# Linear attention and a gated feed-forward on one core: a new order of steps, with most tail loads moved to SyncE's queue

## The chip, the core and the metric

The kernel runs on one core of a Trainium2 chip. Five engines work side by side, each through its own list of instructions in order: PE (matrix products), DVE (vector), ACT (scalar functions and copies), POOL (here almost only an issuer of DMAs) and SP (SyncE, which only issues DMAs). They wait for each other and for DMAs through semaphores. The metric is the device time of one execution in microseconds, as the median of several runs.

## What is computed

```python
# q, k, v: (8 batches, 8 heads, 576 rows, 64), float32
q_p, k_p = phi(q), phi(k)              # phi(x) = where(x > 0, x, exp(x) - 1) + 1
kv  = einsum('bhsd,bhse->bhde', k_p, v)
z   = sum(k_p, axis=2)
num = einsum('bhsd,bhde->bhse', q_p, kv)
den = einsum('bhsd,bhd->bhs', q_p, z)[..., None] + 1e-06
x   = (num / den).transpose(0, 2, 1, 3).reshape(4608, 512)
out = ((x @ w1) * (x @ w2) @ w3) @ w_out     # w1, w2: 512x1024, w3: 1024x1024, w_out: 1024x512
```

The output is 4608x512 in float32.

## The kernel before

Each batch has 576 rows. The first 512 of them are its main part, handled as four blocks of 128 (j = 0 to 3); the last 64 are its tail. The main part of q, k or v of one batch is loaded in two halves of 512 KB (four heads each), the tail in small DMAs of 64 KB: four for q and k together, two for v. A chunk of the feed-forward is the 512 main rows of one batch (chunks 0 to 7); chunk 8 is made of all eight tails. w3 and w_out are multiplied together at the start, so that the second half of the feed-forward is one product with `wf_sb`.

All work is written as steps, and a table (`ORDER`) lists them in the order in which they are recorded. Scheduling is manual: each engine executes its instructions in the order of the table, and a step puts instructions into several engines' lists at once. A `+` behind a step chooses the other engine: POOL and not SP for a load, DVE and not ACT for most copies. The steps that matter here, with batch or chunk b:

- `Lb.g`, `Mb.g`, `Nb.g`: load half g of k, q, v (`load_qkv`, L104). `Rb.0` and `Rb.1`: load the tails of q and k, and of v (`load_tail`, L114). The buffers are pools of 13 halves and of 3 tails of each kind; a load waits for the buffer's last reader.
- `x`, `y`, `z` (k) and `X`, `Y`, `Z` (q): the three parts of phi on ACT (L179) and DVE (L184, L204, L209). `vb.i`: cast of a v half (L215) or tail (L221).
- `Kb`: the product of k and v of a batch (`kvp`, L245, L249) and its copy to `kv` (L254). It needs both halves and the tails of k and v of its batch.
- `Tb.0`: transpose of phi(q) by a DMA on SP (L269). `Ab.j`: one block of rows times kv (`nd`, L310), divided on DVE (L324 to L326); j = 4 is the tail. `Db.p`: transpose of the result by a DMA on SP (`xt`, L351).
- `Fc.f`: one eighth of the gated first layer of chunk c, eight matmuls into `a_ps` and `b_ps` (L362), an ACT copy (L367) and a DVE product (L368). Chunks 6, 7 and 8 use other steps for it, `Gc.q.i`: Strassen-like units of four or eight matmuls (L422), whose sums and products run on ACT (L450, L458) and DVE (L454, L459, L465). `e` and `d` make the sums of weights and of x that they need (L396, L407).
- `Oc.m`: one quarter of the second layer (eight matmuls into `o_ps`, L536, and a copy, L538). `S`, `H` and `Q` store the output.

PE, DVE and ACT take their work from the same table, and so do the two issuers of DMAs. SP's queue holds the halves, the transposes and the stores in the order of the table; when the DMA at its head waits for a buffer or for data, all behind it wait as well. POOL's list after the start holds only tails. So a tail on POOL never stands in front of a half or of a transpose in its issuer's list, and a tail on SP does.

`GATES` adds two waits by hand: the load `R6.0` waits for the landing of `T3.0`, and `M2.1` for `B0.0`.

Of the kernel before, what the change touches and what calls it, by code (L numbers as in the profile page):

```python
# [20 lines left out]
def kernel(  # L21
# [568 lines left out]
    A3.2 F2.0 M5.1 Y5.1 R5.1+ R4.1+ y4.2 S1.1 F2.2 M4.1 A3.1 R5.0+ D3.0 x4.2 z4.2 M4.0 F2.1 Y4.1  # L590
    N4.1 F2.4 R6.1+ L4.1 e0.0 A2.4 v4.2 L4.0 F2.6 e0.2 F2.7 X5.1 Z5.1 A3.4 F3.3 X4.0 Y4.0 Z4.0 O2.3+
    X4.1 y5.2 v4.1 y4.1 F3.1 y6.2 Z4.1 x4.1 F3.4 z4.1 v5.2 y4.0 x4.0 F3.0 N4.0 z4.0 F3.5 v4.0 O2.2+
    M5.0 X5.0 K4 v6.2+ e0.1 T4.0 F3.7 x5.2 z5.2 L5.1 x5.1 Y5.0 Z5.0 y5.1 F3.2 S0.0 A4.1 F3.6 L5.0
    y5.0 O2.1 N5.0 x5.0 A4.0 v5.0 O2.0 z5.1 N5.1 S2.1 A4.2 T5.0 v5.1 O3.3 z5.0 A4.3 D4.0 O3.2+ K5
    S3.1 O3.1 A5.3 M6.1 O3.0 A5.0 F4.0 X6.1 A5.2 F4.7 M6.0 X6.0 Y6.0 Z6.0 D3.1 F4.2 F4.4 A5.1 F4.5
    e1.0 F4.3 L6.1 y6.1 x6.1 A4.4 R7.0 L6.0 y6.0 y7.2 D5.0 F4.1 x6.0 F4.6 z6.0 Y6.1 Z6.1 F5.6 x6.2
    z6.2 z6.1 F5.5 N6.1 v6.1 N6.0 A5.4 e1.1 e1.3 M7.0 X7.0 F5.7 S2.0 F5.4 Y7.0 O4.2+ v6.0 K6 O4.3
    T6.0 A6.3 S3.0 O4.0 A6.1 F5.3 D5.1 x7.2 z7.2 A6.0 M7.1 Y7.1 R7.1 X7.1 Z7.1 N7.0 v7.0 L7.0 F5.1
    F5.0 A6.2 L7.1 Z7.0 F5.2 x7.1 y7.1 O4.1 y7.0 A6.4 e0.3 x7.0 z7.0 S4.1 z7.1 O5.0+ v7.2 N7.1 v7.1
    D6.0 d6.2 O5.1 K7 d6.0 d6.1 d6.3 G6.1.1 e1.2 T7.0 G6.0.1 G6.0.2 G6.1.2 m6.0.2 G6.1.3 G6.0.3  # L600
    G6.1.4 A7.3 S4.0 G6.0.4 G6.0.5 G6.1.5 S5.0 G6.2.4 G6.0.6 G6.0.7 G6.1.6 G6.1.7 m6.1.6 A7.0 m6.0.6
    G6.2.1 G6.2.2 G6.3.1 G6.2.3 G6.3.2 G6.3.3 G6.2.5 G6.3.4 G6.2.6 G6.3.5 G6.2.7 A7.4 G6.3.6 G6.3.7
    O5.2 m6.3.2 D1.1 A7.2 O5.3 m6.1.2 m6.2.6 D7.1 d8.0 d8.1 d8.3 G8.0.1 G8.0.2 d8.2 A7.1 G8.1.1
    G8.0.3 m6.3.6 G8.0.4 G8.1.3 G8.0.5 m8.0.5 G8.1.4 m6.2.5 G8.3.4 S5.1 D7.0 G8.1.5 G8.0.7 m6.2.2
    G8.2.4 G8.0.6 m8.0.6 G8.1.7 O6.0 m6.3.5 m6.1.5 m6.0.5 O6.3 d7.2 G8.2.1 G8.2.2 m8.2.2 d7.0 G8.3.1
    G8.2.3 G8.1.6 G8.3.3 G8.2.5 G8.3.2 G7.0.4 G8.3.5 G8.2.7 G8.3.6 m8.3.6 m8.1.6 G7.1.4 G8.3.7
    m8.0.2 O6.2+ S6.1 d7.1 d7.3 O6.1 S6.0 m8.2.5 G7.0.1 m8.3.5 G8.1.2 m8.1.5 m8.1.2 G7.1.1 G7.0.3
    G7.0.6 G7.1.3 G7.0.5 G7.2.4 G7.1.5 G8.2.6 G7.0.7 G7.1.6 G7.1.7 G7.0.2 m8.2.6 m8.3.2 m7.1.6
    G7.2.1 G7.2.2 G7.3.1 G7.2.3 G7.3.2 m7.0.5 G7.3.4 G7.3.3 G7.2.5 G7.3.6 G7.3.5 G7.2.7 G7.1.2
    G7.2.6 G7.3.7 m7.0.2 m7.2.5 O8.2 O8.3 m7.3.2 H8.3 m7.3.5 m7.2.2 O8.0 m7.1.2 m7.0.6 O8.1+ H8.2  # L610
    S8.0 O7.0 O7.1 S7.0 m7.2.6 m7.3.6 m7.1.5 O7.2+ H7.2 Q7.3
# [118 lines left out]
```

## Time and profile before

| | us |
|---|---|
| Median of 3 runs (248.71 to 250.32) | 249.44 |
| Profiled execution, whole | 247.36 |
| Its span, first to last instruction | 245.6 |
| PE busy | 229.7 (94%) |
| DVE busy | 184.7 (75%) |
| ACT busy | 136.4 (56%) |
| POOL busy | 44.8 (18%) |
| HBM traffic | 38.80 MB read, 9.44 MB written, 196 GB/s over the span |
| SP's queue (q1) | 36.71 MB, 55.4% of 16 DMA engines |
| POOL's queue (q0) | 12.33 MB, 25.1% of 16 DMA engines |

Busy time is the union of an engine's instructions; a PE that the page shows as busy has matmuls in flight, which need not be a PE without small waits. The span is counted from the first instruction; the profiled execution is 1.8 us longer than its span. All windows below are microseconds from the span's start.

### The profile page before, as it was taken

To read this page: it belongs to the slowest core of one execution; us is meant where nothing else is said; L and a number is where in the kernel's file an instruction comes from. 1 tells how busy PE (TensorE), PEld (TensorE's weight loads), DVE (VectorE), ACT (ScalarE), POOL (GpSimd) and SP (SyncE) were. 2 spreads that over 40 slices of the span, in tenths; PEclk is the share of its full clock that TensorE was granted. 3 is DMA by queue.
4 is the path that set the end of the run, shared out by engine and by line. 5 is a ranking of instruction groups with operands and counts; after the bars stand their busy time and mean duration, and the time that the engine had idled before them with its cause. 6 is when DMAs were issued, how large, how long until landed. Compare 5 with 4: busy or idle time off the path is not lost.

```text
span 245.6 us, 4278 instructions
## 1 busy us (share of the span) xinstructions
PE 229.7 (94%) x1548; PEld 133.2 (54%) x1548; DVE 184.7 (75%) x425; ACT 136.4 (56%) x222; POOL 44.8 (18%) x73
## 2 busy tenths in 40 slices
PE   0689968999999999999999999999999999999994
PEld 0345555654454554444545444454498686788542
DVE  3227979677698837989794589958999996989721
ACT  2207777658775715498663456736776285455220
POOL 8445467660000096200000000000000000000000
PEclk9999997999999999999999999999999999999999
DMA  6999999999869799798997989989980151040074
GB/s 152 192 201 299 297 250 243 198 274 280 274 126 350 152 247 313 166 348 225 275 308 153 256 221 242 280 231 328 209 247 0 23 144 29 0 175 0 3 171 171
DMA packets 65461, 49.43 MB, mean 201 GB/s; under 512 B 34016, under 2 KB 60384, under 8 KB 65440
## 3 DMA queue, kind: packets, MB, share of 16 engines
q1 hardware_dynamic: 54560, 36.71, 55.4%
q0 software_dynamic: 10736, 12.33, 25.1%
q8 instruction: 12, 0.20, 0.3%
q10 hardware_dynamic: 144, 0.13, 0.2%
q14 instruction: 9, 0.07, 0.1%
HBM read 38.80 MB, written 9.44 MB: 196 GB/s over the span
## 4 chain that ended last, share of the span: by engine, by line
PE 83%; DMA 13%; ACT 2%; issue 1%; POOL 0%; ACTq 0%; POOLq 0%
PE o_ps L536 25%; PE a_ps L362 17%; PE b_ps L362 17%; PE gu L422 9%; PE gt L422 6%; DMA q<-in_q_dram 5%; DMA k<-in_k_dram 5%; PE nd L310 4%; DMA wt_sb<-in_moe_w_out_dram 3%; PE kvp L245 2%; ACT e L179 1%; PE o_ps L561 1%; PE kvp L249 1%; PE xtp L341 1%; POOL w3b L137 0%
## 5 line engine op out<-in xcount | busy, mean ns | idle before, releaser
L536 PE MATMUL o_ps<-wf_sb,ab 128*128 128x512 bf16 x280 | 64.7, 379 | 0.0
L362 PEld LDWEIGHTS <-w_sb 128*128 128x128 bf16 x384 | 36.6, 98 | 40.2 <-issue 0.6
L362 PE MATMUL a_ps<-xt,w_sb 128*128 128x512 bf16 x192 | 50.8, 382 | 0.0
L362 PE MATMUL b_ps<-xt,w_sb 128*128 128x512 bf16 x192 | 50.2, 379 | 0.0
L536 PEld LDWEIGHTS <-ab 128*128 128x128 bf16 x280 | 26.9, 98 | 29.1 <-DVE ab L465 0.3
L368 DVE TENSOR_TENSOR ab<-a_sb,b_ps 128x512 bf16<-128x512 f32 x48 | 32.4, 684 | 13.0 <-PE b_ps L362 6.5
L367 ACT COPY a_sb<-a_ps 128x512 f32<-128x512 f32 x48 | 27.5, 585 | 21.5 <-PE a_ps L362 20.2
L538 ACT COPY o_sb<-o_ps 128x512 f32<-128x512 f32 x27 | 15.6, 586 | 34.6 <-PE o_ps L536 24.9
L326 DVE TENSOR_TENSOR xn<-nd,r 128x512 bf16<-128x512 f32 x30 | 20.7, 691 | 1.0
L422 PEld LDWEIGHTS <-spare 128*128 128x128 bf16 x192 | 18.6, 97 | 2.4
L179 ACT ACTIVATE e<-q 128x1024 bf16<-128x1024 f32 x16 | 16.8, 1058 | 5.0 <-DMA q<-in_q_dram 4.9
L310 PE MATMUL nd<-kv,qt 128*128 128x130 bf16 (+1 forms) x160 | 15.9, 221 | 2.8 <-DVE xn L326 1.7
L454 DVE TENSOR_TENSOR spare<-spare,gt 128x512 f32<-128x512 f32 x24 | 16.0, 682 | 2.8 <-ACT spare L450 2.3
L310 PEld LDWEIGHTS <-qt 128*128 128x128 bf16 (+1 forms) x160 | 11.5, 99 | 11.6 <-DVE xn L326 3.0
L154 PE MATMUL wf_ps<-wt_sb,w3t 128*128 128x512 bf16 x64 | 16.1, 394 | 1.1 <-DMA wt_sb<-in_moe_w_out_dram 0.8
L179 ACT ACTIVATE e<-k 128x1024 bf16<-128x1024 f32 x16 | 16.9, 1060 | 0.2 <-DMA k<-in_k_dram 0.2
L450 ACT COPY spare<-gu 128x512 f32<-128x512 f32 x24 | 13.4, 590 | 3.4 <-PE gu L422 2.8
L422 PEld LDWEIGHTS <-w_sb 128*128 128x128 bf16 x144 | 14.0, 98 | 2.4
L465 DVE TENSOR_TENSOR ab<-spare 128x256 bf16<-128x256 f32 x36 | 13.7, 419 | 0.1
L114 POOL DMA_DIRECT2D qk32r<-in_q_dram x12 | 7.6, 636 | 33.5 <-ACT o_sb L538 30.9
L324 DVE TENSOR_SCALAR r<-nd 128x8 f32<-128x8 f32 (+1 forms) x38 | 6.1, 162 | 10.0 <-PE nd L310 9.9
L209 DVE TENSOR_TENSOR qj<-e,y 128x512 bf16<-128x512 bf16 x32 | 12.1, 421 | 1.7 <-ACT e L179 0.9
(87 smaller groups left out, 301.9 us busy)
## 6 DMA issues: line engine op xcount, KB each, us to landing
out_dram<-o_sb SPq DMA_DIRECT2D x15, 512.0 KB, 4.3
q<-in_q_dram SPq DMA_DIRECT2D x13, 512.0 KB, 6.8
k<-in_k_dram SPq DMA_DIRECT2D x12, 512.0 KB, 6.9
v<-in_v_dram SPq DMA_DIRECT2D x12, 512.0 KB, 7.7
w3b<-in_moe_w_dram POOLq DMA_DIRECT2D x8, 256.0 KB, 10.1
k<-in_k_dram POOLq DMA_DIRECT2D x4, 512.0 KB, 8.5
w_sb<-in_moe_w_dram POOLq DMA_DIRECT2D x8, 256.0 KB, 7.8
q<-in_q_dram POOLq DMA_DIRECT2D x3, 512.0 KB, 11.0
```

Of the source, the lines that this page charges most:

```text
L154: nc.tensor.matmul(wfs[i], w3ts[i][:, kc, :], wo_sb[:, kc, :], start=(kc == 0), stop=(kc == FC - 1))
L179: nc.scalar.activation(out=e, in_=x, func=AF.Exp)
L310: nc.tensor.matmul(nds[g][rows, i * 2 * E1:(i + 1) * 2 * E1], w, kvs[b % 2][:, i, g].rearrange("p u e -> p (u e)"), start=True, stop=True)
L326: nc.vector.tensor_tensor(out=dst.rearrange("p (g h) e -> p g h e", g=2), in0=v4[:, :, :, 0:D], in1=r[rows].unsqueeze(3).to_broadcast([n, ...
L362: nc.tensor.matmul(ps, w[:, kc, f * P:(f + 1) * P], xt_of(c)[:, :, kc, :], start=(kc == 0), stop=(kc == KC - 1))
L367: nc.scalar.copy(out=a_sb, in_=a_ps)
L368: nc.vector.tensor_mul(out=abs_[c][:, f, :], in0=a_sb, in1=b_ps)
L422: nc.tensor.matmul(t[:, w], l, r, start=(first and w == 0 and k == 0), stop=(k == 1), skip_group_check=True)
L454: nc.vector.tensor_tensor(out=s, in0=o, in1=t, op=ALU.add)
L465: (nc.gpsimd if alt else nc.vector).tensor_mul(out=abs_[c][:, f, r * HN:(r + 1) * HN], in0=s[:, 0], in1=s[:, 1])
L536: nc.tensor.matmul(o_ps, ab[:, f, m * P:(m + 1) * P], wf_sb[:, f, :], start=(f == 0), stop=(f == FC - 1))
L538: copy_of(alt)(out=rows_of(c, m // 2)[:, m % 2], in_=o_ps)
```

## The change

Only the table changes. It keeps its 594 steps, and the first 165 of them are as they were (up to `x2.2`, behind the first two gated units of chunk 1). From there the steps stand in another order, and 28 of them have the other engine flag. Eight tail loads lose their `+` and so move from POOL to SP: `R2.1`, `R3.1`, `R4.0`, `R4.1`, `R5.0`, `R5.1`, `R6.0`, `R6.1`. Only `R2.0` and `R3.0`, which stand before the cut, stay on POOL; `R7.0` and `R7.1` were on SP already. Of the copies and casts, `O2.2`, `O2.3`, `O3.2`, `O4.2`, `O6.2`, `O7.2`, `O8.1`, `v2.1` and `v3.2` go from DVE to ACT, and `O1.1`, `O3.0`, `O3.1`, `O5.1`, `O6.3`, `O8.2`, `v4.0`, `v6.1`, `v7.0`, `v7.1` and `K7` from ACT to DVE. `GATES` stays.

```diff
-    A1.4 x2.1 F1.7 F1.6 x2.2 y2.2 z2.2 N2.1 y3.2 x3.2 O0.3 F1.0 Y2.0 X2.0 Z2.0 N2.0 y2.1 F1.1 v2.1+
-    R2.1+ z2.1 L2.0 y2.0 v2.2 F1.5 R3.1+ x2.0 z2.0 M3.0 v2.0 F1.4 O0.2 X3.0 K2 Y3.1 v3.2+ Z3.1 O0.1
...
+    A1.4 x2.1 F1.7 F1.6 x2.2 L2.0 y2.1 z2.1 M3.0 O0.3 X2.0 y2.2 F1.4 N2.0 N2.1 x2.0 O0.0 z2.2 x3.2
+    Y2.0 Z2.0 y2.0 R2.1 F1.1 Y3.1 Z3.1 v2.0 T2.0 z2.0 v2.1 y3.2 F1.2 Y3.0 L3.0 v2.2 L3.1 X3.0 z3.2
...
```

What this does to the lists of the issuers is clearest between the transposes of q of batch 4 and of batch 5. On SP, before (qt is the transpose of q, k32 and v32 are halves, out_0_dram the store of an output):

```order
L269 DMA_TRANSPOSE qt_1553<-qj_1308 128x18x128
L104 DMA k32_1571<-in_k_dram 128x4x256
L546 DMA out_0_dram<-o_sb_1010 128x1024
L104 DMA k32_1618<-in_k_dram 128x4x256
L104 DMA v32_1633<-in_v_dram 128x4x256
L104 DMA v32_1660<-in_v_dram 128x4x256
L546 DMA out_0_dram<-o_sb_1434 128x1024
L269 DMA_TRANSPOSE qt_1672<-qj_1393 128x18x128
```

and in the changed kernel (qk32r and v32r are tails):

```order
L269 DMA_TRANSPOSE qt_1475<-qj_1295 128x18x128
L104 DMA k32_1518<-in_k_dram 128x4x256
L104 DMA k32_1542<-in_k_dram 128x4x256
L114 DMA qk32r_1599<-in_q_dram 64x4x64 x2
L114 DMA qk32r_1599<-in_k_dram 64x4x64 x2
L546 DMA out_0_dram<-o_sb_1179 128x1024
L104 DMA v32_1619<-in_v_dram 128x4x256
L114 DMA v32r_1633<-in_v_dram 64x4x64 x2
L104 DMA v32_1648<-in_v_dram 128x4x256
L269 DMA_TRANSPOSE qt_1653<-qj_1472 128x18x128
```

Between the two transposes stand six tail DMAs more, all of them ahead of the last v half of batch 5, and one store less. POOL's list ended with these tails before; none of its rows is left in the changed kernel:

```order
L114 DMA qk32r_1103<-in_q_dram 64x4x64 x2
L114 DMA qk32r_1103<-in_k_dram 64x4x64 x2
L114 DMA qk32r_1144<-in_q_dram 64x4x64 x2
L114 DMA qk32r_1144<-in_k_dram 64x4x64 x2
L114 DMA v32r_1266<-in_v_dram 64x4x64 x2
L114 DMA v32r_1269<-in_v_dram 64x4x64 x2
L114 DMA qk32r_1299<-in_q_dram 64x4x64 x2
L114 DMA qk32r_1299<-in_k_dram 64x4x64 x2
L114 DMA v32r_1342<-in_v_dram 64x4x64 x2
```

These are the tails of batches 4, 5 and 6; the v tails of batches 2 and 3, which stood ahead of them, are gone from POOL as well, and those of batch 7 are on SP in both kernels. The third place is DVE's list in the G units of chunk 6. Before (gu_2408 is the bank into which units 5 and 7 of quarter 2 write on PE; spare are operands and sums, ab products, nd, r and xn the division of one block of attention):

```order
L326 TENSOR_TENSOR xn_2342<-nd_2398,r_2403 128x512
L465 TENSOR_TENSOR ab_2290<-spare_2301 128x256
L454 TENSOR_TENSOR spare_2299<-spare_2299,gt_2414 128x512
L454 TENSOR_TENSOR spare_2298<-spare_2298,gt_2431 128x512
L454 TENSOR_TENSOR spare_2296<-spare_2301,gu_2408 128x512
```

and in the changed kernel, where the same bank is gu_2401:

```order
L326 TENSOR_TENSOR xn_2326<-nd_2386,r_2391 128x512
L454 TENSOR_TENSOR spare_2278<-spare_2278,gt2_2340 128x512
L454 TENSOR_TENSOR spare_2280<-spare_2279,gt2_2346 128x512
L454 TENSOR_TENSOR spare_2282<-spare_2277,gt_2418 128x512
L465 TENSOR_TENSOR ab_2271<-spare_2282 128x256
L465 TENSOR_TENSOR ab_2271<-spare_2280 128x256
L454 TENSOR_TENSOR spare_2277<-spare_2281,gu_2401 128x512
```

Between the division and the addition that reads this bank stand two products and three additions, where one product and two additions stood.

More of the change, by code (lines that the diff above doesn't have):

```diff
@@ L585 @@
     M2.1 M3.1 A1.3 F0.3 P1.3 X2.1 R2.0+ A1.0 L2.1 h0 h1 Y2.1 P1.0 M2.0 h2 h3 Z2.1 i0 i1 X3.1 R3.0+
-    A1.4 x2.1 F1.7 F1.6 x2.2 y2.2 z2.2 N2.1 y3.2 x3.2 O0.3 F1.0 Y2.0 X2.0 Z2.0 N2.0 y2.1 F1.1 v2.1+
-    R2.1+ z2.1 L2.0 y2.0 v2.2 F1.5 R3.1+ x2.0 z2.0 M3.0 v2.0 F1.4 O0.2 X3.0 K2 Y3.1 v3.2+ Z3.1 O0.1
-    Y3.0 Z3.0 T2.0 A2.3 F1.2 A2.2 N3.0 F1.3 v3.0 L3.1 z3.2 L3.0 x3.0 x3.1 y3.0 S0.1 y3.1 O0.0 N3.1
-    T3.0 A2.1 R6.0+ v3.1 O1.1 z3.0 A2.0 O1.0 D2.0 R4.0+ S1.0 z3.1 K3 O1.2 A3.0 O1.3 A3.3 F2.5 F2.3
@@ L590 @@
[L590 to L611, printed above, removed]
+    A1.4 x2.1 F1.7 F1.6 x2.2 L2.0 y2.1 z2.1 M3.0 O0.3 X2.0 y2.2 F1.4 N2.0 N2.1 x2.0 O0.0 z2.2 x3.2
+    Y2.0 Z2.0 y2.0 R2.1 F1.1 Y3.1 Z3.1 v2.0 T2.0 z2.0 v2.1 y3.2 F1.2 Y3.0 L3.0 v2.2 L3.1 X3.0 z3.2
@@ new lines @@
+    Z3.0 F1.0 K2 e0.0 R3.1 O0.1 A2.3 x3.0 O0.2 A2.1 S0.0 y3.0 F1.3 A2.2 v3.2 N3.1 y3.1 F1.5 N3.0
+    T3.0 A2.0 x3.1 z3.1 v3.1 z3.0 O1.1+ e1.0 v3.0 D2.0 O1.0 e1.1 e1.3 S1.0 K3 O1.2 D1.1 A3.1 M4.1
+    O1.3 A3.2 F2.0 A3.0 F2.7 F2.1 X4.1 e1.2 A3.3 e0.2 M4.0 X4.0 F2.6 Y4.0 Z4.0 F2.3 A2.4 F2.2 F2.4
+    Y4.1 Z4.1 L4.1 x4.1 y4.1 z4.1 R4.0 F2.5 N4.0 v4.0+ x4.2 S0.1 y4.2 z4.2 D3.0 M5.1 X5.1 R4.1 F3.0
+    v4.2 L4.0 y4.0 x4.0 z4.0 A3.4 F3.2 Y5.1 O2.2 N4.1 M5.0 F3.3 Z5.1 T4.0 v4.1 F3.1 Y5.0 X5.0 Z5.0
+    K4 L5.0 O2.3 A4.3 x5.0 L5.1 F3.5 A4.2 F3.7 y5.0 z5.0 x5.1 F3.4 R5.0 y5.2 x5.2 z5.2 S1.1 A4.1
@@ new lines @@
+    N5.0 v5.0 O2.0 R5.1 v5.2 O2.1 N5.1 y5.1 v5.1 T5.0 A4.0 D4.0 S2.0 S2.1 z5.1 F3.6 K5 O3.2 A5.1
+    R7.1 O3.3 M6.1 A5.2 F4.6 F4.7 A5.3 O3.0+ L6.0 y6.0 F4.0 Y6.1 A5.0 F4.1 X6.1 Z6.1 M6.0 x6.0 Y6.0
+    e0.1 e0.3 X6.0 F4.2 F4.3 z6.0 O3.1+ Z6.0 A4.4 F4.5 R6.1 v6.2+ L7.1 x7.1 L6.1 y7.1 D5.0 F5.3 M7.1
+    Y7.1 X7.1 N6.0 Z7.1 F5.0 R6.0 y6.2 v7.2 A5.4 S3.1 x6.2 z6.2 F5.2 y6.1 N6.1 v6.0 v6.1+ F4.4 x6.1
+    z6.1 F5.5 F5.6 K6 L7.0 y7.0 O4.2 T6.0 A6.0 N7.0 z7.1 M7.0 F5.7 S3.0 Y7.0 D5.1 R7.0 N7.1 A6.2
@@ new lines @@
+    X7.0 Z7.0 O4.1 O4.0 S4.0 v7.0+ x7.2 A6.1 y7.2 z7.2 F5.1 A6.3 x7.0 z7.0 F5.4 D6.0 O4.3 v7.1+ A6.4
+    T7.0 O5.0+ d6.0 d6.1 O5.1+ d6.3 G6.0.1 d6.2 K7+ G6.1.1 G6.1.2 m6.1.2 S5.0 G6.0.3 A7.3 G6.1.3
+    G6.0.4 G6.1.4 G6.0.5 G6.1.5 G6.2.4 G6.0.2 G6.0.7 G6.1.7 A7.0 G6.0.6 D3.1 G6.2.1 G6.1.6 G6.3.1
+    G6.3.2 G6.2.3 m6.3.2 m6.1.6 G6.3.3 G6.3.4 G6.2.5 G6.3.5 A7.4 G6.2.7 m6.3.5 G6.2.6 G6.3.7 G6.2.2
+    A7.2 D7.1 d8.0 d8.1 m6.2.2 d8.3 O5.2 d8.2 O5.3 m6.1.5 G8.1.4 G8.0.1 A7.1 S5.1 m6.0.5 G8.1.1
+    G8.1.2 m6.0.2 G8.0.3 G8.1.3 G8.0.4 m6.2.5 G8.0.5 G8.2.4 G8.1.5 G8.1.6 G8.0.7 S4.1 G6.3.6 m6.3.6
@@ new lines @@
+    G8.1.7 m6.0.6 m6.2.6 D7.0 d7.0 G8.0.2 d7.1 d7.3 d7.2 O6.0 O6.3+ G8.2.1 G8.0.6 G8.2.2 m8.2.2
+    G8.3.1 m8.1.6 G8.2.3 G8.2.6 G8.3.3 G8.2.5 G8.3.4 G7.1.4 m8.0.5 G8.3.5 G8.2.7 G8.3.2 m8.3.2
+    G7.0.4 m8.1.5 G8.3.7 m8.0.6 m8.0.2 m8.1.2 O6.2 m8.2.5 O6.1 G7.0.1 m8.3.5 G7.0.2 m7.0.2 G7.1.1
+    G7.0.3 S6.0 G7.0.6 S6.1 G7.1.3 G7.0.5 G7.2.4 G7.1.5 G7.0.7 G7.1.6 G7.1.7 G8.3.6 m8.3.6 G7.2.1
+    G7.2.2 G7.3.1 m8.2.6 G7.2.3 G7.2.6 m7.2.2 G7.3.3 G7.2.5 G7.3.4 G7.1.2 G7.3.5 G7.2.7 G7.3.2
+    G7.3.6 G7.3.7 O8.2+ H8.2 O8.3 m7.3.6 H8.3 O8.0 m7.2.5 m7.0.5 O8.1 m7.1.5 S8.0 m7.0.6 m7.2.6
@@ L612 @@
+    m7.1.2 m7.3.2 O7.0 O7.1 m7.3.5 S7.0 m7.1.6 O7.2 H7.2 Q7.3
     """
```

## The prediction, written before the result

> **What bounds the kernel now.** I read the page's head first, then the busy time by stretches, then the chain.
>
> ```profile
> span 245.6 us, 4278 instructions
> PE 229.7 (94%) x1548; PEld 133.2 (54%) x1548; DVE 184.7 (75%) x425; ACT 136.4 (56%) x222; POOL 44.8 (18%) x73
> PEclk9999997999999999999999999999999999999999
> ...
> 100.00:140.00 40.00, 40.00 (x237) 20.15 (x236) 31.22 (x72) 24.69 (x39) 0.00 (x0) 1.00 0.95 255
> 140.00:180.00 40.00, 40.00 (x236) 20.08 (x234) 34.63 (x77) 25.17 (x39) 0.00 (x0) 1.00 0.96 250
> 180.00:228.00 48.00, 48.00 (x401) 37.94 (x400) 44.05 (x99) 27.03 (x53) 0.00 (x0) 1.00 0.22 68
> ```
>
> The stretch rows give PE, PEld, DVE, ACT and POOL busy, then granted clock, DMA share and GB/s. PE is busy without a gap and at full clock. Behind it stand two nearly full resources: the DMA engines (0.95 and 0.96 up to 180 us), and DVE after 180 us (44.05 of 48). A busy PE might still hide small waits, so I lay the chain between two key/value products against the work in it:
>
> ```profile
> 117.41 0.45 PE kvp L245 x8
> ...
> 129.81 1.73 PE o_ps L536 x8
> 131.54 0.45 PE kvp L245 x8
> ```
>
> An output unit is 1.73 us, an F unit (four a_ps and four b_ps matmuls at the same spacing) also 1.73, a product of K about 1.13, an A unit 0.23. Between K4 (117.41) and K5 (131.54) stand K4 itself, three F, four O and four A: 1.13 + 7 x 1.73 + 4 x 0.23 = 14.16 against 14.13 elapsed. So there is nothing to win in the steady part. The change keeps every matmul; it can only uncover waits that the old order hides. All that it touches lies behind 60 us; the starting phase, with its slower clock slice, is not touched.
>
> **The change, part by part.** Steps on PE: the same multiset, so 0. What matters is when a step is due against when its inputs arrive. Counting the steps ahead of each K with the prices above: K2, K3 and K6 are due when they were. K4 and K5 are due 3.46 us sooner, K4 because one F and one O fewer stand ahead of it, K5 because two O fewer do. K7 is due one G unit later.
>
> Eight tails move from POOL to SP: three of q and k (4 DMAs each) and five of v (2 each), 22 DMAs. POOL's issue time that goes was hidden, and no one gains from it. On SP they stand between the halves. The first place where that counts is the run from T4.0, the transpose of q of batch 4, to K5, which needs both v halves of batch 5.
>
> ```profile
> 113.06 2.68 SPq L269 DMA_TRANSPOSE qt<-qj  x1
> 115.79 0.58 SPq L104 DMA_DIRECT2D k<-in_k_dram  x1
> 119.04 0.65 SPq L104 DMA_DIRECT2D v<-in_v_dram  x1
> ...
> qt<-qj SPq DMA_TRANSPOSE x1, 4.6
> k<-in_k_dram SPq DMA_DIRECT2D x1, 512.0 KB, 4.8
> v<-in_v_dram SPq DMA_DIRECT2D x1, 512.0 KB, 8.1
> ...
> 128.57 1.06 ACT L215 CAST vt<-v 128x1024 bf16<-128x1024 f32 x1
> ```
>
> The second three rows are the times from issue to landing of the first three. The transpose lands at 117.7, the first k half at 120.6, the last v half at 127.1. Three steps of the queue (store, k, v) and the last v lie between the last two: 6.5 / 4 = 1.6 us for each 512 KB. The last half then needs its cast (1.06, with some 0.2 around it), so K5 could start at 128.4 and starts at 131.54: **3.1 us to spare**. After the change the same five 512 KB pieces stand there with six tails between them. What is a tail worth in line? The trace has two places where SP carries some:
>
> ```profile
> 136.98 0.60 SPq L104 DMA_DIRECT2D k<-in_k_dram  x1
> 137.76 1.85 SPq L114 DMA_DIRECT2D qk32r<-in_q_dram  x2
> 139.65 1.28 SPq L114 DMA_DIRECT2D qk32r<-in_k_dram  x2
> 140.97 0.61 SPq L104 DMA_DIRECT2D k<-in_k_dram  x1
> ...
> k<-in_k_dram SPq DMA_DIRECT2D x1, 512.0 KB, 6.5
> k<-in_k_dram SPq DMA_DIRECT2D x1, 512.0 KB, 7.0
> q1 hardware_dynamic: 1040, 0.28, 127.6%
> ...
> 160.60 0.57 SPq L104 DMA_DIRECT2D q<-in_q_dram  x1
> 161.28 1.30 SPq L114 DMA_DIRECT2D v32r<-in_v_dram  x2
> 162.63 0.60 SPq L104 DMA_DIRECT2D v<-in_v_dram  x1
> ...
> q<-in_q_dram SPq DMA_DIRECT2D x1, 512.0 KB, 4.5
> v<-in_v_dram SPq DMA_DIRECT2D x1, 512.0 KB, 6.2
> ```
>
> First place: the k halves before and behind four tails land at 143.5 and 148.0; less 1.6 for the half itself, 2.9 us, or 0.72 a tail. Second place: q at 165.1, v at 168.8, less 1.6, so 2.1 for two tails, or 1.06. Low end: from 142.6 to 143.7, while nearly only tails moved, the queue row shows 0.28 MB; at 64 KB that is 4.3 tails in 1.1 us, which the share of 127.6% stretches to 1.4: 0.33 a tail. Range for six tails: 2.0 to 6.4. I take 0.72, the place with the most tails: 4.3.
>
> T4.0 helps a little: it stood behind K4 in the code and now stands one F unit ahead of it, so its issue, now 4.35 us ahead of K4, can come 0 to 1.7 sooner; I take 0.85. K4 to K5 hold 14.1 us of PE work as before. K5: 3.1 + 0.85 - 4.3 = -0.35, so **PE loses 0.4 us there**; bounds 0 (spare 2.8) and 3.3.
>
> A rule speaks on that price. The Trainium skill (DMA: Bandwidth & Descriptors, Specifications) puts the smallest transfer for line rate at 512 B and says that less means a read-modify-write; a doubled low end would be an estimate of 0.66 a tail, and K5 would just hold. The trace can be asked, since POOL's tails travel in larger packets than SP's:
>
> ```profile
> q0 software_dynamic: 105, 0.22, 107.0%
> ```
>
> Between 93.0 and 94.0 us that is 2.1 KB a packet and 1.07 / 0.22 = 4.9 engine shares for a MB; SP's 1040 packets of 270 B cost 1.1 x 1.276 / 0.28 = 5.0. So here the small packets cost no more to move, against the rule.
>
> At K3 (batch 3) two v tails stand ahead and both v halves have become last, where one was.
>
> ```profile
> 73.67 0.38 SPq L104 DMA_DIRECT2D v<-in_v_dram  x1
> v<-in_v_dram SPq DMA_DIRECT2D x1, 512.0 KB, 7.6
> ...
> 84.96 0.62 PE L245 MATMUL kvp<-vt,kj 128*128 128x130 bf16 x8
> ```
>
> Landed 81.3, K3 at 84.96, cast and edges 1.3: 2.4 to spare. Two tails at 0.72 (0.33 to 1.06) and a second cast of 1.06 behind the first take 1.7 to 3.2: covered at my price, 0.8 lost at the high one.
>
> After 180 us DVE is full, so its order decides. The wait is that of unit 7 of quarter 2 of chunk 6 on the DVE addition that reads the same bank.
>
> ```profile
> 186.14 0.39 PE L310 MATMUL nd<-kv,qt 128*128 128x130 bf16 x4
> ...
> 190.78 0.60 PE L422 MATMUL gu<-spare,w_sb 128*128 128x256 bf16 x4
> ...
> 188.52 0.41 DVE L465 TENSOR_TENSOR ab<-spare 128x256 bf16<-128x256 f32 x1
> 188.85 1.28 DVE L454 TENSOR_TENSOR spare<-spare,gt 128x512 f32<-128x512 f32 x2
> 190.04 0.68 DVE L454 TENSOR_TENSOR spare<-spare,gu 128x512 f32<-128x512 f32 x1
> ```
>
> The addition ends at 190.72, the unit starts at 190.78: no spare. In the new order three additions and two products stand between the scaling of nd and this addition, where two and one stood: 0.60 + 0.33 more (spacings of these rows). PE has 4.64 us from nd to the unit now; then ten groups of 0.44, the nd products and a 64-row nd, about 5.05, or 0.4 more. That leaves 0.5 late, less up to 0.4 if the scaling starts sooner than the 1.3 us behind its nd that it takes now: **0.1 to 0.5, taken as 0.3**. Other places there trade alike; I put nothing on them.
>
> The engine flags: seven output copies go from DVE to ACT and six the other way, net three more 128x1024 casts on DVE and K7's copies. DVE is idle for 8.8 and 5.4 us in the two stretches before 180 us, which hides it; without that cover it would cost under 2 us. Weight sums (e steps) on DVE move forward into 75 to 125 us, same cover.
>
> **Sum**: 0.4 + 0.3 = 0.7. On the profiled execution, 247.36 (its span 245.6 plus 1.8 around it), 248.1. The median shown, 249.44, is 2.1 above that execution, so the forecast for a median is **250.1**.
>
> **Rivals.**
>
> 1. Slower: a tail in line is worth about 1.06 everywhere. K5: 3.1 + 0.85 - 6.4 = 2.5 lost, K3 0.8, DVE's 0.3: 253.0, with K7's v tails up to 254. For it: the second in-line place, and DMA at 0.95. Against: the first place and the packets' own time. It starts to cost at 0.66 a tail at K5 and decides beyond about 0.95.
>
> 2. No net cost: tails only change lanes, each costs its 0.33, K5 keeps 2.8 us, and DVE's 0.3 is lost or won back elsewhere: 249.4 to 249.7. The rows that carry it, of 86.3 to 99.1 us, when POOL's tails ran beside SP's transfers:
>
> ```profile
> q1 hardware_dynamic: 3012, 2.52, 68.5%
> q0 software_dynamic: 467, 0.97, 32.9%
> ```
>
> Both queues filled the same engines (101% together), so the tails took their share from the halves already. The Trainium skill (DMA: Bandwidth & Descriptors, Issuing engines are not separate DMA queues) says just that: DMAs of all issuers run on the same 16 engines and interleave. The trace agrees with these 101%. What stands against it is that in line a tail delays the half behind it, not all transfers alike.
>
> 3. Faster: the 2.1 us between profiled execution and median are waits on late transfers that come and go, and a single queue ends them: down to 247.4. Nothing in the profile shows such waits, and more than 1% (below 246.9) would need less time than the profiled execution, whose PE has no gap.
>
> **How the numbers follow.** Forecast (249.8 to 251.8) 0.47; rival 1 0.26; rival 2 0.19; rival 3 0.08. About 1% (246.9 to 251.9) is what a measurement of this kernel tells from no change. Slower by over 1%: rival 1 and the upper edge of the forecast, 0.28. Faster by over 1%: the far half of rival 3, 0.04. Within: 0.68. The range leaves out a tenth at each end: 248.3, between rivals 2 and 3, to 253.4, in rival 1.
>
> **What would show it.** Right: SP's k halves of batch 5 and its v halves lie some 4 us further apart around the tails; K5's first matmul (L245) waits on ACT's vt or vr by 0 to 1 us; POOL issues no DMA after 53 us; the G stage shows one wait on DVE's L454 of some 0.3. Wrong: an unbroken PE and a span of 245.6 or less (rival 2 or 3), or gaps at several kvp or at the first gu of chunk 6 (rival 1). I would be wrong outright if the transposes of SP (L269, L351), and not the halves, came late behind the tails: then nd and a_ps would wait, at a price that no row here gives.

## The result, and the profile after

The changed kernel takes 250.07 us, the median of 20 runs (249.06 to 252.07), beside 248.63 us for the kernel before, also of 20 runs. The ratio is 1.0076, with a 95% interval of 1.0055 to 1.0097. A second set, of 12 (e8 below), gave 249.08 us and 1.0031 (0.9999 to 1.0063). Over both sets the difference of the means is 1.35 us, plus or minus 0.40. So the change costs some 0.5%. Ratios and differences here and below leave out a few outlying executions (three of before, of 250, 311 and 492 us, one of e6, of 251 us, and one of e12, of 848 us).

From the page of the changed kernel, its head and the busy engines (time, share of the span, instructions):

```profile
span 248.2 us, 4260 instructions
PE 229.5 (92%) x1530; PEld 133.0 (54%) x1548; DVE 187.2 (75%) x427; ACT 134.3 (54%) x220; POOL 31.9 (13%) x51
```

The same stretches as before the change (length, then PE, PEld, DVE, ACT, POOL busy, the clock, the DMA share and GB/s):

```profile
100.00:140.00 40.00, 39.84 (x233) 20.01 (x235) 31.52 (x71) 23.63 (x39) 0.00 (x0) 1.00 1.00 256
140.00:180.00 40.00, 39.84 (x217) 19.13 (x219) 34.52 (x77) 21.41 (x33) 0.00 (x0) 1.00 1.04 235
180.00:228.00 48.00, 47.61 (x399) 37.58 (x401) 44.02 (x99) 26.07 (x51) 0.00 (x0) 1.00 0.31 81
```

POOL issues no DMA after 53.8 us, and the DMA engines are as full as they were. PE is still busy nearly everywhere, at full clock. (18 matmul records are missing from this trace, 1530 of 1548, and each leaves a gap of 0.05 us that is no wait.) Busy shares say too little here, so I measured from matmul start to matmul start, which gives four stretches of the execution. All times are us; "last" is the last matmul:

| | K2 starts at | K2 to K3 | K3 to K6 | K6 to last | last to end of span |
|---|---|---|---|---|---|
| before | 72.42 | 12.55 | 75.25 | 81.51 | 3.84 |
| changed | 73.64 | 12.69 | 75.32 | 82.28 | 4.27 |
| changed, second profile (e8) | 74.01 | 12.86 | 75.25 | 82.58 | 4.27 |

The spans differ by 2.6, but 1.2 of it is the start of K2. This start lies anywhere from 72.4 to 75.1 in the profiles of the kernels here, and through the 48 matmuls ahead of K2 PE goes at the same pace (10.36 us). The lists of all engines are the same up to 50.7 us (SP's is the first to differ), and K1, which starts at 44.35 in before and at 45.57 in the changed kernel, is already 1.2 apart; it is scatter, and not the change. The rest, 0.14 + 0.07 + 0.77 + 0.43, is 1.4 us (1.8 in the second profile), as much as the times of the first set say (the second set says 0.9, plus or minus 0.6). So three places remain to be explained: K3, the G stage, and the part behind the last matmul. K4 and K5, at which the prediction saw more than half of the loss, show nothing.

### The profile page after: what moved, and what is told of

The parts are those of the page before. It is cut to its first block, busy times and chain, and to the rows that moved or that the text cites. A ratio compares the mean times of both kernels' runs of the same rounds, so it can differ in the third digit from the quotient of the medians.

```text
span 248.2 us, 4260 instructions
## 1 busy us (share of the span) xinstructions
PE 229.5 (92%) x1530; PEld 133.0 (54%) x1548; DVE 187.2 (75%) x427; ACT 134.3 (54%) x220; POOL 31.9 (13%) x51
## 4 chain that ended last, share of the span: by engine, by line
PE 81%; DMA 12%; DVE 2%; ACT 1%; issue 1%; POOL 0%; ACTq 0%; DVEq 0%; POOLq 0%
PE o_ps L536 24%; PE a_ps L362 17%; PE b_ps L362 17%; PE gu L422 8%; DMA w3b<-in_moe_w_dram 8%; PE gt L422 6%; DMA q<-in_q_dram 4%; PE nd L310 4%; PE kvp L245 2%; ACT e L179 1%; PE o_ps L561 1%; PE xtp L341 1%; PE kvp L249 1%; PE kvp L239 0%; ACT xt L342 0%
## 5 line engine op out<-in xcount | busy, mean ns | idle before, releaser
L536 PE MATMUL o_ps<-wf_sb,ab 128*128 128x512 bf16 x265 | 62.3, 379 | 0.8
L538 ACT COPY o_sb<-o_ps 128x512 f32<-128x512 f32 x28 | 16.1, 586 | 31.2 <-PE o_ps L536 23.0
L450 ACT COPY spare<-gu 128x512 f32<-128x512 f32 x24 | 13.6, 588 | 11.1 <-PE gu L422 11.1
L454 DVE TENSOR_TENSOR spare<-spare,gt 128x512 f32<-128x512 f32 x24 | 16.0, 680 | 1.9 <-ACT spare L450 1.8
L147 PE MATMUL w3p<-ident,w3b 128*128 128x128 bf16 x64 | 6.3, 266 | 8.9 <-DMA w3b<-in_moe_w_dram 8.9
L422 PE MATMUL gu<-spare 128*128 128x256 bf16 x96 | 13.3, 272 | 0.0
```

The source lines that it names most:

```text
L422: nc.tensor.matmul(t[:, w], l, r, start=(first and w == 0 and k == 0), stop=(k == 1), skip_group_check=True)
L450: nc.scalar.copy(out=s, in_=t)
L454: nc.vector.tensor_tensor(out=s, in0=o, in1=t, op=ALU.add)
L536: nc.tensor.matmul(o_ps, ab[:, f, m * P:(m + 1) * P], wf_sb[:, f, :], start=(f == 0), stop=(f == FC - 1))
L538: copy_of(alt)(out=rows_of(c, m // 2)[:, m % 2], in_=o_ps)
```

## The experiments

e8 is the changed kernel again, without an edit, on the chip of e5, e6 and e7; its numbers stand above.

> The changed kernel itself, unaltered, beside the three others on the same chip. 1.0055 to 1.0097 of before again; K6 to the last matmul 82.2 to 82.3; K2 to K3 anywhere from 12.7 to 13.2, since with the same front two other kernels gave 12.69 and 13.15.

The ratio of 1.0031 is lower than expected, and the 82.58 from K6 on is more.

Theory A: the loss is a sum of small waits, at a K or an xt that comes late and in DVE's new order of the G stage. Theory B: the tails in SP's queue are the whole loss. Theory C: the tails make the transposes late, which costs much more.

### One part of the change at a time (e1, e2)

e1 is the kernel before with the eight tails moved to SP in their old places, and without the wait of `R6.0` for `T3.0`:

```diff
-    T3.0 A2.1 R6.0+ v3.1 O1.1 z3.0 A2.0 O1.0 D2.0 R4.0+ S1.0 z3.1 K3 O1.2 A3.0 O1.3 A3.3 F2.5 F2.3
+    T3.0 A2.1 R6.0 v3.1 O1.1 z3.0 A2.0 O1.0 D2.0 R4.0 S1.0 z3.1 K3 O1.2 A3.0 O1.3 A3.3 F2.5 F2.3
...
-    GATES = "R6.0<T3.0 M2.1<B0.0"
+    GATES = "M2.1<B0.0"
```

> The order of before, with the eight tails on SP in their old places, and without the wait of R6.0 for T3.0. Theory A (the loss of the change is several small waits: a K or an xt that comes late because tails stand in line, and new waits of DVE's order in the G stage): here DVE's order is the old one, so no new G wait. In line four tails (R6.0) stand ahead of D2.0, whose result landed 0.6 us before its first use in before; at 0.3 a tail that is 1.2, so about 0.6 lost there; K5, with nothing new ahead of it, loses nothing. 0.3 to 1 us slower than before. Theory B (the move of the tails is the whole loss): as the changed kernel, 1.0055 to 1.0097. Theory C (the eight tails make the transposes late): more than 2 us slower, with nd and a_ps waiting.

e2 is the reverse, the changed order with the eight tails on POOL:

```diff
-    Y2.0 Z2.0 y2.0 R2.1 F1.1 Y3.1 Z3.1 v2.0 T2.0 z2.0 v2.1 y3.2 F1.2 Y3.0 L3.0 v2.2 L3.1 X3.0 z3.2
+    Y2.0 Z2.0 y2.0 R2.1+ F1.1 Y3.1 Z3.1 v2.0 T2.0 z2.0 v2.1 y3.2 F1.2 Y3.0 L3.0 v2.2 L3.1 X3.0 z3.2
...
```

> The changed order with the eight tails on POOL. Theory A: K3's wait of 0.19 and the wait of 0.17 of the first G unit for its xt go, the G stage's waits on DVE (0.25 and 0.2) stay: 0.3 to 0.4 us faster than the changed kernel, still 0.4 to 0.6 slower than before (ratio to before about 1.002 to 1.004). Theory B: as before, 0.999 to 1.001, and the G waits gone or without effect. If the tails on POOL are dearer than in line: slower than the changed kernel.

Measured: e1 253.45 us (4 runs), 1.0183 (1.0147 to 1.0218) of before; e2 249.86 us, 1.005 (1.0021 to 1.0078). Theory B falls on both sides. The move alone, in the old order, costs 4.8 us, three times the loss of the change; and the new order without the move loses nearly as much as with it. The new order is in part what makes the move bearable.

e1's loss has the size of C, but most of it has another way. From its timeline (start, length, engine, line, operation; what the engine waited for in brackets):

```profile
83.94 1.29 SPq L114 DMA_DIRECT2D qk32r<-in_q_dram  x2
85.27 1.27 SPq L114 DMA_DIRECT2D qk32r<-in_k_dram  x2
86.65 1.50 SPq L351 DMA_TRANSPOSE xt<-xn  x1
88.33 1.89 SPq L114 DMA_DIRECT2D qk32r<-in_q_dram  x2
90.27 1.27 SPq L114 DMA_DIRECT2D qk32r<-in_k_dram  x2
91.64 0.55 SPq L546 DMA_DIRECT2D out_dram<-o_sb  x1
...
95.53 1.07 ACT L538 COPY o_sb<-o_ps 128x512 f32<-128x512 f32 x2 [8.33 <-DMA out_dram<-o_sb]
...
91.26 1.02 PE L362 MATMUL a_ps<-xt,w_sb 128*128 128x512 bf16 x4 [0.95 <-DMA xt<-xn]
...
97.15 1.16 PE L362 MATMUL a_ps<-xt,w_sb 128*128 128x512 bf16 x3 [2.04 <-ACT a_sb L367]
```

SP needs 0.6 us to issue one tail DMA, and here it has no backlog that would hide it: the transpose of x waits behind four of them (PE loses 0.95), and the store of an output block behind eight. The store frees one of the two output buffers, ACT's next copy wants it and waits 8.33 us, and ACT's list is in order, so the copies of a_ps behind it come late and PE loses 2.04. (Much later, at 176.70, it waits 0.50 for such a copy once more.) Then the clock falls as well (a stretch, columns as above):

```profile
97.00:101.00 4.00, 3.85 (x11) 1.42 (x11) 2.71 (x6) 1.17 (x3) 0.00 (x0) 0.57 0.96 283
```

Behind the wait the granted clock is 0.57 for four microseconds, which costs another 1.7.

### The G stage (e3, e5, e11)

e3 keeps the changed kernel up to D6.0 and takes the old order from there. e5 is the reverse, but with K7 on ACT and ahead of the first G unit, as before; e11 is e5 again. The edit of e3:

```diff
-    T7.0 O5.0+ d6.0 d6.1 O5.1+ d6.3 G6.0.1 d6.2 K7+ G6.1.1 G6.1.2 m6.1.2 S5.0 G6.0.3 A7.3 G6.1.3
+    T7.0 O5.0+ D3.1 S4.1 d6.2 O5.1 K7 d6.0 d6.1 d6.3 G6.1.1 G6.0.1 G6.0.2 G6.1.2 m6.0.2 G6.1.3
...
```

> The changed kernel up to the transpose of chunk 6 (D6.0), then the order of before from the sums d6 on; the tails stay on SP. Theory A: the waits of the G stage on DVE (0.25 at unit 7 of quarter 2, 0.2 at the o_ps behind it) go, K3's 0.19 and the first G unit's 0.17 stay: 0.4 to 0.5 us faster than the changed kernel, 1.001 to 1.004 of before. Theory B: the G stage's waits cost nothing, so as the changed kernel, 1.0055 to 1.0097. If the G waits are made by something ahead of the stage and not by the order in it, they come again with the old order.

> The order of before up to D6.0 and through K7 (d6.2 O5.1 K7, as before), then the order of the changed kernel from d6.0 on; the tails of before, so the eight on POOL. From K6's first matmul to the last matmul before took 81.51 us, the changed kernel 82.28. Theory A (the order of the G stage makes most of the loss, on DVE): 82.0 to 82.2, since the two waits on DVE (0.25 and 0.21) come again and the wait for xt (0.17) doesn't; K2 to K3 as before (12.55). Time 1.002 to 1.004 of before. Theory B' (the median's loss of 1.4 to 1.9 us needs the front and the back together, or something the profile doesn't show): 1.000 to 1.001. If the back half alone makes the whole measured loss: 1.0055 or more.

> The same kernel as e5 (old front, G stage of the changed kernel), for a second profile and a second median, since its first median was as before although its stretch from K6 to the last matmul was 0.85 us longer. If the waits of the G stage are in every execution: the stretch again 82.3 to 82.4, and over both sets of runs 0.3 to 0.8 us slower than before. If they are only in the profiled one: a stretch nearer 81.5.

| | K2 to K3 | K6 to last | last to end | median | ratio to before |
|---|---|---|---|---|---|
| e3 | 13.15 | 81.50 | 4.34 | 248.52 | 1.0001 (0.9972 to 1.0029) |
| e5 | 12.54 | 82.36 | 3.79 | 248.25 | 1.0001 (0.9971 to 1.0031) |
| e11 | 12.55 | 82.25 | 3.79 | 249.02 | 1.003 (0.9998 to 1.0061) |
| e2, above | 12.86 | 82.33 | 3.80 | 249.86 | 1.005 (1.0021 to 1.0078) |

The stretch from K6 on is 81.5 with the old order (before, e3, e7) and 82.2 to 82.6 with the new one in seven profiles, with tails on SP and with tails on POOL. Three lie elsewhere: e1, in the old order, has 82.16, with its late wait of 0.50 ahead of the G stage; e4 (below), whose queue is late throughout, has 84.46; and e9 (below), in the new order, has 81.98. So the 0.8 us come with the order of the G stage, but not all of them every time. What they are made of, the chain of the changed kernel shows (start, length, what the time was spent on):

```profile
190.93 0.90 PE gu L422 x8
...
191.87 1.02 DVE spare L454 x2
...
193.35 0.70 DVE xnr L326
...
194.08 0.43 DVE ab L459
...
194.55 0.38 PE o_ps L536
```

For 2.7 us the path to the end leads over DVE: two additions, the division of the tail block, a product. PE waits at both ends. In e3 the same place has PE alone in its chain:

```profile
191.81 0.87 PE gu L422 x8
192.68 0.34 PE nd L310 x4
193.02 0.54 PE gt L422 x4
193.57 0.44 PE gu L422 x4
194.00 1.73 PE o_ps L536 x8
```

The two waits are the predicted one of unit 7 (0.25, at 192.34) and one of O5.2 behind it (0.21, at 194.55): its bank is one that a G unit filled, and the product L459 that reads it now stands behind the division. These two, 0.46 together, stand in every profile with the new order of the G stage. To them come 0.16 for xt at the first G unit (179.84; 0.37 in the second profile) and 0.17 ahead of the nd group at 182.89. The wait for xt is in e2 too (0.21), with the tails on POOL, so the tails do not make it. It is not in e5 and e11, which have K7 ahead of this unit. They pay 0.31 at another place instead (181.7: gu waits for a copy of ACT, L450). This second part changes from profile to profile: e12 has no wait for xt, but one of 0.34 for DVE's copy of an output (209.87), and e9 has neither, so that only 0.5 is left there.

In the times the 0.8 us are at the edge of what can be resolved: e5 and e11 together are 0.32 us, plus or minus 0.45, slower than before. Theory A had e5 at 1.002 to 1.004 and e3 at 1.001 to 1.004, and both came out lower.

### K3: a store, not the tails (e6, e12, e7)

K3 waited 0.19 in the changed kernel, 0.25 in e2, 0.65 in e3, 0.36 in e8. That e2, with the tails on POOL, has it too speaks against the tails. From the timeline of the changed kernel:

```profile
73.92 1.29 SPq L114 DMA_DIRECT2D v32r<-in_v_dram  x2
77.31 0.37 SPq L546 DMA_DIRECT2D out_dram<-o_sb  x1
77.77 1.34 SPq L104 DMA_DIRECT2D v<-in_v_dram  x2
...
85.23 1.05 ACT L215 CAST vt<-v 128x1024 bf16<-128x1024 f32 x1 [0.36 <-DMA v<-in_v_dram]
...
86.33 0.61 PE L245 MATMUL kvp<-vt,kj 128*128 128x130 bf16 x8
```

Behind the tails SP is idle for 2.1 us, from 75.2 to 77.31: the store S0.0 at the head of its queue waits for its output block, and the two v halves of batch 3 stand behind it. In before one store stood there too, but it waited 0.63 (72.60 to 73.23) and one v half had already gone. e6 moves this store behind the halves, e7 does the same to e3, and e12 is e6 again:

```diff
-    Z3.0 F1.0 K2 e0.0 R3.1 O0.1 A2.3 x3.0 O0.2 A2.1 S0.0 y3.0 F1.3 A2.2 v3.2 N3.1 y3.1 F1.5 N3.0
+    Z3.0 F1.0 K2 e0.0 R3.1 O0.1 A2.3 x3.0 O0.2 A2.1 y3.0 F1.3 A2.2 v3.2 N3.1 y3.1 F1.5 N3.0 S0.0
...
```

> The changed kernel with one store (S0.0) moved on SP from ahead of the two v halves of batch 3 to behind them. In the changed kernel SP waited 2.10 us at this store for its o_sb (0.63 in before), and the two v halves stood behind it. Theory A' (this store, and not the tails, makes K3 late): K2 to K3 goes from 12.7 to 13.2 back to 12.5, the wait of K3 on ACT's vt is gone, and the rest stays: 0.2 to 0.6 us faster than the changed kernel. Theory T (the two v tails ahead make K3 late): 0.1 to 0.2 of the wait stays.

> Both together: the changed order up to D6.0 with that store moved, the order of before behind it, the tails on SP. Theory A: K2 to K3 12.5, K6 to the last matmul 81.5, so the steady part is that of before (169.3 from K2 to the last matmul) and the time 0.999 to 1.001 of before. If queueing the tails on SP itself costs or wins something: 0.5 us or more beside that.

> The same kernel as e6 (the changed kernel with S0.0 behind the v halves), for a profile without disturbance and a second median. From K2 to K3 12.5 again, from K6 to the last matmul 82.3 to 82.4, the closing part 4.3. If these add up in the time: 1.0 to 1.4 us slower than before over both sets; if the first median (0.1 slower) was right, something else in the executions of before is as long and its one profile doesn't show it.

From the timeline of e12:

```profile
75.83 1.09 SPq L104 DMA_DIRECT2D v<-in_v_dram  x2
77.79 0.36 SPq L546 DMA_DIRECT2D out_dram<-o_sb  x1
...
83.75 1.98 ACT L215 CAST vt<-v 128x1024 bf16<-128x1024 f32 x2
...
86.64 0.62 PE L245 MATMUL kvp<-vt,kj 128*128 128x130 bf16 x8
```

The casts end at 85.73, 0.9 us ahead of K3, and K2 to K3 is 12.51 in e6, e7 and e12. It is the store: with the two v tails still ahead of the halves nothing of the wait is left. The landing of the last v half, counted from K2's start, shows why: 11.6 to 12.0 us in the changed kernel, e2, e3, e4 and e8, which all wait, and 8.8 to 9.0 in e6, e7 and e12, as in before (8.8). Times: e6 248.62 us, 1.001 (0.9981 to 1.004); e12 249.46 us, 1.0039 (1.0007 to 1.007), together 0.44 plus or minus 0.40 over before; e7 248.84 us, 1.0008 (0.9977 to 1.004). The stretches of e7 are those of before (12.51, 75.25, 81.50) but for the last (4.35). So the eight tails in line cost PE nothing once the store and the G stage are as before. The stretches of e6, and those of e12, are in sum 1.3 us longer than those of before, and the times show 0.44 plus or minus 0.40: here the stretches claim a larger loss than the times. So they do for e3 (1.1 against 0.08 plus or minus 0.58). Before has one profile only, whose steady part has hardly a wait for data (0.14 at 77.36 and 0.11 at 226.25), and which took 247.36 us, 1.3 less than the median; its other executions may have more waits; that is not shown.

### The price of a tail in line (e4)

e4 follows each of the 22 moved DMAs on SP with a twin into a buffer that nobody reads:

```diff
+            u = twin.tile([P, RW], F32, tag="u", name="twin") if 1 < b < 7 and not alt else None
...
                 first = first or ins
+                if u is not None:
+                    nc.sync.dma_start(
+                        out=u[g * R:(g + 1) * R].rearrange("p (h d) -> p h d", d=D),
+                        in_=src[name][b, g * 4:(g + 1) * 4, NJ * P:S, :].rearrange("h p d -> p h d"))
```

> The changed kernel, and each of the 22 tail DMAs that were moved to SP is followed on SP by a twin that loads the same data into a buffer nobody reads (same result, 1.44 MB more read). In the changed kernel the cast ahead of K5 ended 0.1 us before K5, K3 waited 0.19, and 6 tails between the halves took some 0.28 each. Theory A (a tail in line is worth about 0.3): K5 then 1.5 to 1.9 late, K3 0.4 to 0.6 later, so 1.9 to 2.5 us slower than the changed kernel, 1.015 to 1.018 of before. A price of 0.72 a tail: K5 alone 4.2 late, 1.025 or more. No price (tails only share the engines): as the changed kernel.

Measured: 257.31 us, 1.0332 (1.029 to 1.0374): 8.7 us over before and 7.2 over the changed kernel, where 1.9 to 2.5 were expected of a price of 0.3, and 4.2 at K5 of a price of 0.72. Both prices are right, in different places. In the changed kernel (timeline, and between them two rows of the DMA issues with the time from issue to landing, of the first k half and the last v half):

```profile
110.31 3.88 SPq L269 DMA_TRANSPOSE qt<-qj  x1
114.23 1.13 SPq L104 DMA_DIRECT2D k<-in_k_dram  x2
115.54 1.28 SPq L114 DMA_DIRECT2D qk32r<-in_q_dram  x2
116.89 1.26 SPq L114 DMA_DIRECT2D qk32r<-in_k_dram  x2
118.19 0.60 SPq L546 DMA_DIRECT2D out_dram<-o_sb  x1
118.83 0.43 SPq L104 DMA_DIRECT2D v<-in_v_dram  x1
119.31 2.06 SPq L114 DMA_DIRECT2D v32r<-in_v_dram  x2
121.47 0.54 SPq L104 DMA_DIRECT2D v<-in_v_dram  x1
...
k<-in_k_dram SPq DMA_DIRECT2D x1, 512.0 KB, 4.8
v<-in_v_dram SPq DMA_DIRECT2D x1, 512.0 KB, 5.7
...
128.21 1.05 ACT L215 CAST vt<-v 128x1024 bf16<-128x1024 f32 x1
...
129.36 0.62 PE L245 MATMUL kvp<-vt,kj 128*128 128x130 bf16 x8
```

The first k half lands at 119.0, the last v half at 127.2: 8.2 us, where the prediction's row of before had 6.5 for the same store and halves. Six tails cost 1.7 us, 0.28 each. SP issues all of this in 7.8 us, within the 8.2 that the transfers need, so its 0.6 for each tail is hidden. With six twins more SP's issue is the longer of the two, 12.9 us, and the first k half and the last v half of e4 land 12.6 us apart: each further tail costs 0.74. Then PE waits 2.52 in the middle of K5, and the clock falls again (a row of e4's timeline, and a stretch):

```profile
134.08 0.39 PE L251 MATMUL kvp<-vt,kj 128*128 128x130 bf16 x4 [2.52 <-ACT vt L221]
...
134.20:138.30 4.10, 4.10 (x22) 1.91 (x21) 0.69 (x1) 1.06 (x3) 0.00 (x0) 0.60 1.09 287
```

Wait and clock at K5 make 4.7 of the 9.1 us that e4 takes longer than the changed kernel from K2 to the last matmul. The rest is eight smaller waits of 0.3 to 1.1 us, for data that comes late.

The Trainium skill (DMA: Bandwidth & Descriptors, Issuing engines are not separate DMA queues) says that initiating DMAs on several engines saves only the sequencer's time, which is usually small beside the DMA itself. Beside the 3.9 to 5.4 us from issue to landing of the four tails of q and k in the rows above, 0.6 us of issue is indeed small. Beside what a tail takes of the queue it is not: 0.28.

### Behind the last matmul (e9)

All eight profiles of kernels with the eight tails on SP have 4.1 to 4.4 us from the last matmul's start to the end of the span, and the five with tails on POOL (e10, below, among them) 3.8 to 3.9. The difference sits in one of POOL's closing steps. e9 is the changed kernel with one tail back on POOL:

```diff
-    Y7.1 X7.1 N6.0 Z7.1 F5.0 R6.0 y6.2 v7.2 A5.4 S3.1 x6.2 z6.2 F5.2 y6.1 N6.1 v6.0 v6.1+ F4.4 x6.1
+    Y7.1 X7.1 N6.0 Z7.1 F5.0 R6.0+ y6.2 v7.2 A5.4 S3.1 x6.2 z6.2 F5.2 y6.1 N6.1 v6.0 v6.1+ F4.4 x6.1
```

> The changed kernel with one of the eight tails, R6.0 (4 DMAs), put back on POOL. In the closing sequence behind the last matmul the last but one step of POOL is 0.41 to 0.43 us from the one ahead of it in all seven kernels whose eight tails are on SP (POOL's list has 69 rows there), and 0.06 in all three with them on POOL (98 rows). If the closing 0.4 us come from POOL having been silent since about 60 us, they go here, where POOL issues DMAs at about 148 us, and the last matmul to the end is 3.8 us. If they hang on the length of POOL's list, which is only some ten rows longer here, either may come. If neither matters, 4.3 us.

Measured, in one execution of 250.13 us: the last matmul to the end is 3.76 us, and POOL's step is 0.06 and not 0.41.

Four DMAs on POOL are enough. They were issued at 89 to 92 us and not at 148, since POOL runs ahead of the table; so POOL has been silent for 150 us here as well, and silence is not the whole cause. What it is, and whether it is the length of POOL's list, stays open. K3 had no wait in this profile, with the store where the changed kernel has it: the last v half landed 11.35 us behind K2's start, just early enough. So the store takes away the margin, and the scatter of the landing decides whether K3 waits. From K3 to K6 this execution took 76.05, 0.8 more than the others, with waits for a division (0.54 at 121.01), an xt (0.18 at 106.50) and a copy; whether the tail on POOL makes them is not shown.

### A kernel that beats both (e10)

What is left of lost time in before is a pause of 0.097 us ahead of and behind each group of 64-column matmuls of a tail block. From the timeline of before:

```profile
99.95 1.03 PE L362 MATMUL b_ps<-xt,w_sb 128*128 128x512 bf16 x4
100.90 0.25 PEld L310 LDWEIGHTS <-qt 128*64 128x64 bf16 x4 [0.42 <-DVE y L184]
100.90 0.41 PE L310 MATMUL nd<-kv,qt 128*64 128x130 bf16 x4
101.25 1.04 PE L362 MATMUL a_ps<-xt,w_sb 128*128 128x512 bf16 x4
```

e10 is before with the tail blocks made from 128 columns; the layout of q and its tails in their tile changes with it:

```diff
-                w = qts[b, 1][:, i, g * R:(g + 1) * R]
-            nc.tensor.matmul(nds[g][rows, i * 2 * E1:(i + 1) * 2 * E1], w,
+                at = (0 if b % 2 == 0 else NB * P) + (2 * i + g - b % 2) * R
+                w = qts[b].rearrange("p n t -> p (n t)")[:, at:at + P]
+            nc.tensor.matmul(nds[g][:, i * 2 * E1:(i + 1) * 2 * E1], w,
...
```

> An attempt at a kernel that beats both: before, with the matmuls of the tail blocks (A with j = 4) made from 128 columns of the transposed q and not from 64. In both kernels PE loses 0.097 us ahead of each such group of four 64-column matmuls and 0.097 behind it, with nothing waited for, and these are nearly all that is left of lost time. The tail of even batches is put ahead of the main part of q in its tile, so that 64 more columns of real data always stand beside the wanted ones; the 64 extra rows of the result are not read. Theory: the pause comes with the width of the loaded columns, so all of them go: 6 x 0.19 = 1.2 us behind K2 (K2 to the last matmul 168.1 and not 169.3) and up to 0.4 ahead of it, 0.994 to 0.996 of before. Rival: the pause is that of the other destination or of the switch between kinds of work, and stays: as before.

Measured: 247.36 us, 0.9956 (0.9919 to 0.9993) of before. From the timeline of e10:

```profile
100.98 1.03 PE L368 MATMUL b_ps<-xt,w_sb 128*128 128x512 bf16 x4
101.63 0.43 PEld L316 LDWEIGHTS <-qt 128*128 128x128 bf16 x4
101.84 0.39 PE L316 MATMUL nd<-kv,qt 128*128 128x130 bf16 x4
102.07 1.03 PE L368 MATMUL a_ps<-xt,w_sb 128*128 128x512 bf16 x4
```

From b_ps to nd it is now 0.86 and not 0.95, and from nd on 0.23 and not 0.35. The pauses are gone, all of them. The PEld rows, the loads of the weights, show what changed: in before the first load of the group starts together with its matmuls (100.90), and in e10 0.21 ahead of them, under the matmuls in front. A load of 64 columns takes no less time than one of 128 (0.108 us on average in before, beside 0.097). The Trainium skill (TensorE: Matmul & The Clock Gate, Weight-path perf modes) says that the fast load of weights is on when there are 128 of them; these rows agree, and put a price on the lack of it. The number of output rows grew as well, from 64 to 128, and no run separates the two. In the profiled execution K2 to the last matmul is nevertheless 169.5 (before 169.3, expected 168.1): PE now waits 0.28 for an xt and 0.16 and 0.39 for ACT's copies between 94 and 117 us, where it had not (1.3 us in all, from matmul start to matmul start). Its whole time, 248.25, lies above the median, so I rest the gain on the times and not on this profile.

## Why the prediction was right, and where it was not

The number is right, 250.1 against 250.07, and so is the forecast that the time stays within 1%. The way to it is half right, and part of the agreement is luck. The predicted loss was 0.7 us on a median of three, 249.44; the measured one is 1.4 on a median of 20, 248.63. A loss too small by half and a base too high by 0.8 met in the sum.

- **What bounds the kernel: right.** K4 to K5 takes 14.20 us in the changed kernel by its rows, against 14.16 worked out. K3 to K6 is 75.25 to 75.32 in both.
- **K5, 0.4 lost: wrong, nothing is lost**, though the place was the right one: the last cast ends at 129.26 and K5 starts at 129.36, so the 3.1 us to spare are gone. Three terms were mis-sized and cancel. The price of a tail: 0.28 and not 0.72, which gives back 2.6. The step that failed there is the reading of the first in-line place: the two k halves around four tails were issued 3.99 us apart (136.98 and 140.97), so most of the 2.9 us was SP's issue, and not transfers. So the sign that was named, halves some 4 us further apart, came out as 1.7 (8.2 against 6.5). T4.0: not 0.85 sooner; it landed 0.45 behind K4 in before and 1.1 behind it now, since its issue took 3.88 and not 2.68 us. That takes 1.5. The cast: it waited for a copy on ACT, and from landing to K5 it was 2.2 and not 1.3, which takes 0.9. From -0.35 these lead to about -0.1, and no wait shows.
- **K3, covered: wrong in part.** The tails were covered there, as said. The wait, from none to 0.65, comes with a store in SP's queue that the step did not count; that step went through tails and halves only.
- **The G place, 0.3: right**, 0.25 measured, on DVE's addition L454, as named. "Other places there trade alike; I put nothing on them" is the step that failed: they cost 0.5 more, and G in all 0.8. Of the 0.5, 0.2 stands in every profile of this order.
- **The engine flags, 0: not told apart.** Of K7's copies on DVE the 0.17 ahead of nd at 182.89 may be the trace: it is in e2, e6 and e8 as well, and not in e5 and e11, whose K7 is on ACT; but other steps differ there too.
- **The end behind the last matmul** was not in the sum at all: 0.43.
- **Rival 1** (a tail worth 1.06 everywhere) is refuted for this order: a tail cost 0.28. Where its issuer becomes the bound a tail is dearer (0.74 in e4), though not 1.06. **Rival 2** had the price right, 0.28 beside its 0.33, and K5 without loss. It did not see the rest. **Rival 3** found nothing: no run became faster by the single queue. Nor did the transposes come late behind the tails: nd waits 0.10 us at most for its division, and the one wait for an xt, 0.16, is there with the tails on POOL too.
- **The 512 B rule of the Trainium skill** (DMA: Bandwidth & Descriptors, Specifications), which the prediction held against the trace: at 1.6 us for 512 KB a tail of 64 KB would be 0.2 by its bytes, and it cost 0.28. The four tails of q and k shown under e4 land 0.17 to 0.20 us apart. A doubling is not seen. The packets that the prediction compared do not test the rule, though: POOL's larger ones come from the same rows of 64 floats, 256 B, as SP's.

## What to carry to other kernels

A DMA put into a queue has two prices, the issuer's time and the transfer's share, and in these runs only the larger sum of the two along the queue counted: ask of each place whether the queue has a backlog there. When a load comes late, look at what stands ahead of it in its issuer's list, stores above all, since a store waits for a computation and holds up loads that wait for nothing. And a base from three runs is worth no more than its scatter: here the three lay 1.6 us apart, as much as the effect.
